# Accumulating both row halves of a projection in one PSUM bank, with ten units of queries on chip instead of eight

## The chip, the cores and the metric

The kernel runs on one core of a Trainium2 chip. The metric is device time in microseconds (us) from launch to end. Engines are named as the profile does: PE is TensorE (PEld its weight loads), DVE is VectorE, ACT is ScalarE, POOL is GpSimd, SP is the engine whose queue issues most DMAs.

## The reference

Two attention branches on the same `x` (2048 positions, width 512, 32 heads of 16) are mixed by a gate of each position:

```python
def _A_ref(x, wqkv, wo):          # window of 8 positions, step 2
    qkv = (x @ wqkv).reshape(B, S, 3, H, Dh).transpose(2, 0, 3, 1, 4)
    idx = pos[:, None] - (jnp.arange(8) * 2)[None, :]
    ...
    logits = jnp.einsum("bhsd,bhswd->bhsw", q, kg) * scale
    logits = jnp.where(mask, logits, -1e9)
    return einsum("bhsw,bhswd->bhsd", softmax(logits), vg) ... @ wo
def _B_ref(x, wq, wk, wv, wo):    # 32 query heads, one key and value head
    q, k, v = heads(x @ wq), x @ wk, x @ wv
    p = softmax(einsum("bhqd,bkd->bhqk", q, k) * scale)
    return einsum("bhqk,bkd->bhqd", p, v) ... @ wo
g = sigmoid((x * gate_w).sum(-1, keepdims=True))
return g * _A_ref(x, A_wqkv, A_wo) + (1 - g) * _B_ref(x, B_wq, B_wk, B_wv, B_wo)
```

Branch B is the large one: scores of 2048 x 2048 for 32 heads, with the exact maximum of each row taken off ahead of the exponential.

## The kernel before

The instructions are issued in an order that the program itself works out: it keeps a clock for each engine (`clk`, `free`, and constants such as `T_R` and `T_EXP`) and places work where a buffer should be free by that clock. The chip knows only the resulting order on each engine, and the semaphores between them.

**Units.** Branch B is cut into 32 units: a block of 512 queries and four heads (`NQB` x `NHG`). A unit's queries lie on chip in one of `NB` buffers `qst`, in high and low parts on both halves of the 128 rows. They are projected in the front, written to DRAM (`qd`) and brought to their buffer by `stack(u)` on SP's queue. `home(v)` says which buffer, and after which unit it is free: 8 buffers up to unit 13, then 6, since two of them (`q67`) hold half sums of keys from then on (`half_back` brings those back from DRAM).

**Row halves.** PE runs as two arrays of 64 rows, side by side: a product over 64 rows on rows 0 to 63 can run while another runs on rows 64 to 127. `b` or `odd` is the half in the code.

**The front** (about 24 to 259 us) is a list of 62 row parts (`lumps`): 14 projections of queries ("q", 2 to 15) and 48 of branch A ("a", three column groups of 16 rows blocks). Each is 12 products of 128 x 512 outputs on each half. `stream` gives each half its next product. Half 0 adds up in one PSUM bank, half 1 in the bank beside it, both for the same row part. `queries_post` copies the two banks (ACT), adds them and takes the low part off (POOL); `a_post` copies both and adds them on POOL, or every third time copies one and adds on DVE, and stores to DRAM (`ad`) from four `stage` buffers.

**Maxima.** Before a unit's exponentials, the row maxima of its scores are needed: 64 pieces of 512 keys to a unit, 2048 in all (`NF`). In between its own work, PE computes scores for them: `fill_pair` two at a time into `m2` (two banks, one DVE reduction of 1024), `fill_one` one into `m1` or `po`. Once the half sums and half differences of keys are formed (`half_sel`, `half_keys`, `half_parts`), two pieces of keys go at once: `fill_diff` computes differences and ACT takes their absolute value, `fill_sum` computes sums, and one DVE instruction adds the two and takes the maximum. In the front, `diff_ready` stops new ones at `FRONT` pieces. A unit's finished maxima go through `maxima_turn`, `shift_a` to `shift_d` into its queries' rows.

**PSUM**, eight banks: `eb[0]` and `eb[1]` (two each), `m2` (two), `m1` and `po`. The last row part of the front uses `m2`, so that the first exponentials can use `eb`.

**The main loop** has 512 steps, 16 blocks of 128 keys for each unit. A step issues two `exp_pair` (two score products side by side and one exponential of 128 x 1024 on ACT), the four products of weights and values of the step before (`weighted`, into `po`), one pair of maxima in `m2`, and, as often as `single_share` finds it due, a single one in `m1`. `single_share` spreads what is left over the steps that are left, and holds back while no further unit's queries are on chip. Output rows 0 to 7 and then 8 to 11 are projected in two breaks of the loop (`out_phase`), the last four within the last steps (`spread`). Branch A's own arithmetic runs on POOL throughout (`work`, `a_scores`, `a_values`), from DRAM.

Of the kernel before, what the change touches and what calls it, by code (L numbers as in the profile page):

```python
# [13 lines left out]
P = 128  # L14
# [21 lines left out]
NB = 8  # L36
# [7 lines left out]
FRONT = 468  # L44
# [3 lines left out]
WB = 6  # L48
# [5 lines left out]
class Banks:  # L54


    def __init__(self, tc, name):
        self.tc, self.name, self.pool, self.tiles = tc, name, None, ()
        self.whole()

    def shape(self, n):
        if len(self.tiles) != n:
            if self.pool:
                self.pool.release()
            self.pool = self.tc.alloc_tile_pool(name=self.name + "s", bufs=1, space=PSUM)
# [16 lines left out]
def gated_mix_kernel(ctx, tc, xt, wa, wk, wq, wo_a, wo_b, out):  # L82
# [16 lines left out]
    q67 = cp.tile([P, 2, 2, 512], F32R, name="q67")  # L99
    qst = [cp.tile([P, 2, 512], F32R, name=f"qst{k}") for k in range(NB - 2)] + [q67[:, 0], q67[:, 1]]  # L100
    kd = dp.tile([P, 2, 2, 512], F32, name="kd")
# [7 lines left out]
    eb = [pp.tile([P, 2, 512], F32, name=f"pe{k}") for k in range(2)]  # L109
    m1 = pp.tile([P, 512], F32, name="ps")  # L110
    po = pp.tile([P, 512], F32, name="po")
    m2 = Banks(tc, "pm")

# [25 lines left out]
    wqr = p0.tile([P, C, C, P], F32, name="wqr")  # L139
# [10 lines left out]
    def load_wq(cc, eng):  # L150
        eng.dma_start(wqr[:, cc], wq[:, cc])

    def split_wq(cc):
        cs = slice(cc * P, (cc + 1) * P)
        split(wqh[:, :, cs], wql[:, :, cs], wqr[:, cc])
# [99 lines left out]
    def parts_of():  # L255
        return p0.tile([P, 512], F32R, name="qhi", bufs=3), p0.tile([P, 512], F32R, name="qlo", bufs=2)

    def queries_post(m, bank):
# [3 lines left out]
        two = p0.tile([P, 2, 512], F32, name="two", tag="wqr", bufs=1)  # L262
        nc.scalar.activation(two, bank, AF.Copy)
        at = after("act", clk["pe"] + T_LAT, 0.92)
        own = p0.tile([P, 512], F32, name="qraw", bufs=1)
        nc.gpsimd.tensor_add(own, two[:, 0], two[:, 1])
        pool = max(pool, 1e3 * at) + 1400
        hi, lo = parts_of()

        def rest():  # L270
# [3 lines left out]
            pool = max(pool, 1e3 * after("act", 0, 0.6)) + 1400  # L274
            queries_out(m, hi, lo)
            if m > 4 and m % 2 and len(stacked) < NB:
                stack(len(stacked))

        tasks.append((pool / 1e3, rest, (), "rest"))
# [21 lines left out]
    def a_post(gg, j, x):  # L301

        nonlocal pool
        bank, key = front[x]
        settle("add", 1)
        settle("store", 2)
        own = p1.tile([P, GN], F32, name="stage", bufs=4)
        if gg == 0 and j < 3:
            two = wp.tile([P, GN], F32, name="two", tag="aext", bufs=2)
        else:  # L310
            two = p2[0].tile([P, GN], F32, name="two", tag=("", "raw", "own")[j % 3], bufs=1) if j % 3 else None
        nc.scalar.activation(own, bank[:, 0, :], AF.Copy)
        if two:
            nc.scalar.activation(two, bank[:, 1, :], AF.Copy)
        at = after("act", clk["pe"] + T_LAT, 1.05 if two else 0.52)
        free[key] = at + (0.1 if two else 1.5)

        def rest():
            nonlocal pool
            if two:  # L320
                nc.gpsimd.tensor_add(own, own, two)
                pool = max(pool, 1e3 * at) + 1280
            else:
                nc.vector.tensor_add(own, bank[:, 1, :], own)  # L324
                free[key] = after("dve", at, 0.65) + 0.1

            def store():
                for piece in a_pieces(gg):
                    a_store(own, gg, j, *piece)

            tasks.append((max(pool / 1e3, clk["dve"]) + 0.5, store, (), "store"))
            if j == NJ - 1:
                tasks.append((max(pool / 1e3, clk["dve"]) + 1.0, whole, (gg,)))

        tasks.append((at, rest, (), "add"))
# [17 lines left out]
    stacked, asked = [], set()  # L353
# [14 lines left out]
    slots = [(v, pr, t, kc) for kc in range(2) for v in range(2) for pr in range(2) for t in range(4)]  # L368
    slots += [(v, pr, t, kc) for v in range(2) for pr in range(2) for t in range(4) for kc in range(2, 4)]
    slots += [(v, pr, t, kc) for v in range(2, NU) for pr in range(2) for t in range(4) for kc in range(4)]  # L370
    half = []
    free = {"m2": 0.0, "m1": 0.0, "e0": 0.0, "e1": 0.0, "po": 0.0}
    tasks, shifted, pm = [], set(), []
# [20 lines left out]

    def to_go():
# [14 lines left out]
    def maxima_turn(v, ms):  # L410
        mt = wp.tile([P, 32], F32, name="mt")
        nc.vector.transpose(mt, ms.rearrange("p b x y -> p (b x y)"))
        tasks.append((after("dve", 0, 0.34) + (2.0 if kcd and not pe else 0.1), shift_a, (v, mt)))

    def fill_pair(dst, key):
# [3 lines left out]
        m = unit_tile(v)  # L419
        for odd in range(2):  # L420
# [5 lines left out]
    def fill_one(dst=m1, key="m1"):  # L426
# [4 lines left out]
        m = unit_tile(v)  # L431
        max_mm(dst, v, pr, t, kc, odd)
# [5 lines left out]
    sel, kcd, dd, formed, ended, wants = [], [], [], {}, set(), []  # L438
    hb = {1: (m1, po)}
# [979 lines left out]
```

## Time and profile before

| | us |
|---|---|
| three runs | 1444.36, 1444.67, 1444.96 (median 1444.67) |
| the profiled execution | 1444.01, its span 1442.2 |
| PE busy | 1435.9 |
| ACT busy | 1274.5 |
| DVE busy | 1199.8 |
| POOL busy | 1019.4 |
| first weighted product of the main loop | 259.5 |

The span runs from the first to the last instruction; the executions' time has some 2 us around it. Rows of groups read: line, engine, operation, tile written and tiles read, shapes, count; then busy us and mean ns of one; then the engine's idle time just before them and what ended it. Matmuls overlap, so their busy time is not a measure of how much PE could still take; their count in a stretch is.

### The profile page before, as it was taken

The numbers are of one execution on the slowest core, as the hardware profiler recorded it, in microseconds if no ns is written. First come the engines' busy times: TensorE is split into PE (matmuls) and PEld (weight loads), VectorE is DVE, ScalarE is ACT, GpSimd is POOL, SyncE is SP. The second block draws the span as 40 slices with busy tenths as digits, with TensorE's granted clock in tenths as the row PEclk, the third lists the DMA queues.
The fourth block names the chain that finished last, engine by engine and source line by source line (L and its number), as shares of the span: only waits on it lengthen the run. The fifth ranks groups of instructions, "written<-read, shape, count | busy, mean of one in ns | idle before, by whom it ended". The sixth has DMA issues, their size and how long they took to land.

```text
span 1442.2 us, 29203 instructions
## 1 busy us (share of the span) xinstructions
PE 1435.9 (100%) x10524; PEld 674.7 (47%) x10524; DVE 1199.8 (83%) x1878; ACT 1274.5 (88%) x1596; POOL 1019.4 (71%) x1796
## 2 busy tenths in 40 slices
PE   9999999999999999999999999999999999999998
PEld 7977777433333333333333476333333337333343
DVE  8978889688888888888898888888888888889812
ACT  6659888999999999999999888999999998999986
POOL 7952989878898988888988897888888815111121
PEclk9999999999999999999999999999999999999999
DMA  7753433122021120212322200221202011000110
GB/s 241 220 156 103 130 98 104 56 62 90 14 87 43 46 90 13 72 42 69 97 77 73 85 31 31 83 61 43 72 13 72 12 42 35 9 2 2 28 33 30
DMA packets 107457, 96.12 MB, mean 67 GB/s; under 512 B 84976, under 2 KB 89120, under 8 KB 103088
## 3 DMA queue, kind: packets, MB, share of 16 engines
q1 hardware_dynamic: 100224, 55.04, 14.2%
q0 software_dynamic: 6368, 37.90, 7.9%
q8 instruction: 83, 1.36, 0.4%
q10 hardware_dynamic: 720, 1.31, 0.3%
q14 instruction: 62, 0.51, 0.1%
HBM read 63.18 MB, written 30.49 MB: 65 GB/s over the span
## 4 chain that ended last, share of the span: by engine, by line
PE 99%; DVE 1%; ACT 0%; issue 0%; POOL 0%; DVEq 0%; ACTq 0%; POOLq 0%
PE po L592 35%; PE pe L582 24%; PE pe L1218 12%; PE pm L393 8%; PE ps L393 6%; PE pe L890 5%; PE pm L491 3%; PE ps L491 2%; PE pm L944 1%; PE po L491 1%; PE pe L227 1%; PE po L193 0%; PE po L393 0%; PE pm L1218 0%; PE po L1043 0%; PE ps L1043 0%
## 5 line engine op out<-in xcount | busy, mean ns | idle before, releaser
L584 ACT ACTIVATE pexp<-pe 128x1024 f32<-128x1024 f32 x1022 | 987.2, 1022 | 81.7 <-PE pe L582 78.8
L422 DVE TENSOR_REDUCE mx<-pm 128x2 f32<-128x1024 f32 x508 | 621.0, 1223 | 131.0 <-PE pm L393 125.6
L592 PE MATMUL po<-pexp,vst 128*32 128x512 f32 x4096 | 545.5, 605 | 0.0
L582 PE MATMUL pe<-qst,kst 64*128 64x512 f32 x1916 | 442.2, 451 | 0.4
L582 PEld LDWEIGHTS pe<-qst,kst 64*128 64x128 f32 x1916 | 179.8, 183 | 474.8 <-ACT pexp L584 466.8
L433 DVE TENSOR_REDUCE mx<-ps 128x1 f32<-128x512 f32 x414 | 281.6, 680 | 3.3 <-PE ps L393 3.3
L393 PE MATMUL pm<-kst,qst 62*128 62x512 f32 x980 | 201.3, 396 | 0.1
L656 POOL TENSOR_TENSOR pr<-aext 128x256 f32<-128x256 f32 x256 | 182.0, 737 | 3.0 <-DMA aext<-ad 2.7
L716 POOL TENSOR_TENSOR oa<-oa,av 128x256 f32<-128x256 f32 x224 | 164.0, 732 | 15.4
L393 PE MATMUL ps<-kst,qst 62*128 62x512 f32 x406 | 160.0, 394 | 0.0
L592 PEld LDWEIGHTS po<-pexp,vst 128*32 128x32 f32 x4096 | 80.5, 108 | 166.4 <-issue 157.0
L713 POOL TENSOR_TENSOR av<-aext,lg 128x256 f32<-128x256 f32 x224 | 139.3, 622 | 13.1
L520 ACT ACTIVATE dd<-pm 128x512 f32<-128x512 f32 x180 | 101.5, 606 | 16.4 <-PE pm L491 8.9
L1218 PE MATMUL pe<-wah,xl 64*128 64x512 f32 x376 | 109.9, 393 | 0.0
L1218 PE MATMUL pe<-wal,xh 64*128 64x512 f32 x376 | 108.1, 393 | 0.0
L1218 PE MATMUL pe<-wah,xh 64*128 64x512 f32 x376 | 107.5, 395 | 0.4 <-DVE stage L324 0.3
L393 PEld LDWEIGHTS pm<-kst,qst 62*128 62x128 f32 x980 | 96.9, 186 | 2.8 <-DVE mx L422 0.6
L662 POOL TENSOR_TENSOR tr<-pr 128x512 f32<-128x512 f32 x64 | 81.8, 1278 | 4.4
L520 ACT ACTIVATE pexp<-pm 128x512 f32<-128x512 f32 x116 | 65.0, 600 | 15.3 <-PE pm L491 8.8
L662 POOL TENSOR_TENSOR tr<-tr 128x256 f32<-128x256 f32 (+1 forms) x128 | 72.4, 566 | 8.2
L393 PEld LDWEIGHTS ps<-kst,qst 62*128 62x128 f32 x406 | 75.8, 187 | 3.7 <-issue 1.2
L537 DVE CUSTOM_DVE_ANT_0 dd<-po,dd 128x512 f32<-128x512 f32 x90 | 62.1, 690 | 12.5 <-PE po L491 7.3
(221 smaller groups left out, 1913.8 us busy)
## 6 DMA issues: line engine op xcount, KB each, us to landing
aext<-ad POOLq DMA_DIRECT2D x32, 1056.0 KB, 5.7
qst<-qd SPq DMA_DIRECT2D x60, 128.0 KB
ad<-stage SPq DMA_DIRECT2D x32, 240.0 KB
qd<-qhi SPq DMA_DIRECT2D x16, 256.0 KB
qd<-qlo SPq DMA_DIRECT2D x16, 256.0 KB
td<-raw SPq DMA_DIRECT2D x32, 128.0 KB
oa<-td SPq DMA_DIRECT2D x256, 16.0 KB
xraw<-xt SPq DMA_DIRECT2D x15, 256.0 KB
```

What stands on the lines that cost most here:

```text
L393: nc.tensor.matmul(dst, qst[home(v)[0]][b:b + 62, pr, t * P:(t + 1) * P], kst[b:b + 62, kc * 512:(kc + 1) * 512], start=True, stop=True)
L422: nc.vector.tensor_reduce(m[:, :, pr, t, kc], dst, AX.X, ALU.max)
L433: nc.vector.tensor_reduce(m[:, odd, pr, t, kc:kc + 1], dst, AX.X, ALU.max)
L520: nc.scalar.activation(d[:, odd], m2[:, odd, :], AF.Abs)
L582: nc.tensor.matmul(bank[:, odd, :], kst[b:b + 64, kt * P:(kt + 1) * P], qst[home(u)[0]][b:b + 64, pr, :], start=True, stop=True)
L584: nc.scalar.activation(e, bank, AF.Exp, scale=SCALE)
L592: nc.tensor.matmul(po[32 * i:32 * i + 32, :], vst[:, kt, :], pexp[s, i // 2][:, i % 2, :], start=(kt == 0), stop=(kt == NJ - 1))
L656: nc.gpsimd.tensor_mul(pr[:, k], q, e[:, o:o + NH, AC:2 * AC])
L662: nc.gpsimd.tensor_add(nx, cur[:, :, 0:n], cur[:, :, n:2 * n])
L713: nc.gpsimd.tensor_mul(av, e[:, o:o + NH, 2 * AC:].rearrange("p j (h d) -> p j h d", d=DH), lg[:, w].unsqueeze(3).to_broadcast([P, NH, AG, ...
L716: nc.gpsimd.tensor_add(ao, ao, av)
L1218: nc.tensor.matmul(front[2 if x == last else x % 2][0][:, b, :], l[h], r[h], start=(i == 0), stop=(i == 3 * C - 1))
```

## The change

Both halves of a row part now add up in the same bank. Half 0's 12 products come first, half 1's 12 follow into the same sums; meanwhile half 0 does the next row part. `front_stream` takes the place of `stream` in the front, with four banks, one row part each (`front_bank`). Half 1 may start a row part only once the program's order proves that half 0's last product of it is complete: `mark` notes at each product that waits for a freed bank which earlier products must be done (`known`), and `may` asks for it. One copy by ACT empties a bank; for queries a second copy gives the high part. No addition is left.

`NB` is 10: six buffers of their own and four in branch A's pool (`kept`, `held`), which is laid over the query weights when the query projections are done. Units 6 to 9 are stacked in the first row parts of branch A. `kept` and `held` later serve as an output block and as the second half of branch A's results, so POOL's second pass waits for step 161. The half sums have a buffer of their own (`kcd`), with no way through DRAM. They are formed at "q" 11 and 13 instead of "a" 0, 4 and 0, 6, both in `m2`. `FRONT` is 596 instead of 468. `stage` has two buffers instead of four, `wah` and `wal` have eight instead of six. The second exponential of step 0 is issued after the front's last copy. The first output phase no longer waits for a small lead of the maxima, and a later one waits for it alone.

```diff
-NB = 8
+NB = 10
-FRONT = 468
+FRONT = 596
-WB = 6
+WB = 8
...
-        return (v % NB, v - NB) if v < 2 * NB - 2 else ((v - NB) % (NB - 2), v - NB + 2)
+        return (v % NB, v - NB) if v < 2 * NB - 4 else ((v - NB) % (NB - 4), v - NB + 4)
...
+    eb = [Banks(tc, "pe0", 2, "right"), Banks(tc, "pe1", 2)]
...
     def queries_post(m, bank):
-        nc.scalar.activation(two, bank, AF.Copy)
-        nc.gpsimd.tensor_add(own, two[:, 0], two[:, 1])
+        nc.scalar.activation(own, bank, AF.Copy)
+        nc.scalar.activation(hi, bank, AF.Copy)
         def rest():
-            nc.scalar.activation(hi, own, AF.Copy)
             nc.gpsimd.tensor_sub(lo, own, hi.bitcast(F32))
...
+    def a_post(gg, j, bank):
+        settle("store", 1)
+        own = p1.tile([P, GN], F32, name="stage", bufs=2)
+        nc.scalar.activation(own, bank, AF.Copy)
+        at = after("act", clk["pe"] + T_LAT, 0.52)
...
+    def mark(*keys):
+        known[0] = max([known[0]] + [seen[k] for k in keys if k in seen])
+        seen.update({k: issued[0] for k in keys})
+        issued[0] += 1
...
-            if lump == ("a", 0, 3):
+            if lump == ("q", 10):
                 half_sel()
-            elif lump in (("a", 0, 4), ("a", 0, 6)):
-                wants.append(1 if lump[2] == 4 else 0)
+            elif lump in (("q", 11), ("q", 13)):
+                wants.append(1 if lump[1] == 11 else 0)
...
-        nc.tensor.matmul(front[2 if x == last else x % 2][0][:, b, :], l[h], r[h], start=(i == 0), stop=(i == 3 * C - 1))
+        if b == 0 and i == 0:
+            mark(f"f{x % 4}")
+        nc.tensor.matmul(front_bank(x), l[h], r[h], start=(b == 0 and i == 0), stop=(b == 1 and i == 3 * C - 1))
+        (ends_at if b == 0 else seen)[x if b == 0 else f"f{x % 4}"] = issued[0]
...
+    def may(b, at):
+        x, i = at
+        if b == 0:
+            if i == 0 and x - 4 >= posted[0]:
+                return False
+            lump = lumps[x]
+            return lump[0] == "q" or (lump[1], i // 3) in wal
+        return i > 0 or known[0] >= ends_at[x]
...
+    def front_stream(seq):
+        while min(at) < len(seq):
+            ...
+            for b in sorted((0, 1), key=lambda b: b not in lone):
+                if b in lone:
+                    lone[b]()
+                elif at[b] < len(seq) and (b == 0 or at[0] // n > at[1] // n) and may(b, seq[at[b]]):
+                    dur = max(dur, mm(b, seq[at[b]]))
+                    at[b] += 1
...
+        if lump == ("a", 0, 0) and i == 2:
+            queries_done()
+        if lump[0] == "a" and lump[1] == 0 and lump[2] in (1, 3, 5, 7) and i == 2:
+            stack(len(stacked))
+        if x == last and i == 5:
+            exp_pair(0, 0)
...
+    def queries_done():
+        settle("rest", 0)
+        p0.release()
+        branch_a()
+        for k in range(NB - 4, NB):
+            clear(k, nc.gpsimd)
...
-            yield lambda: g < 8 or p2b
+            yield lambda: (g < 8 or p2b) and (not hf or step[0] > 16 * NB + 1)
...
-        if s == 16 * NB + 4:
-            half_back()
...
-        elif due or ... (lead < LEAD or s >= 16 * (NHG * (k + 2) + 1)):
+        elif due or ... (not outs or lead < LEAD):
```

More of the change, by code (lines that the diff above doesn't have):

```diff
@@ L299, in a_store, with store @@
         nc.sync.dma_start(dst, src)
[L301 to L335, printed above, removed]
+    def a_post(gg, j, bank):
[3 more added lines that the diff above has]
+        at = after("act", clk["pe"] + T_LAT, 0.52)
+        def store():
+            for piece in a_pieces(gg):
+                a_store(own, gg, j, *piece)
+        tasks.append((at + 0.5, store, (), "store"))
+        if j == NJ - 1:
+            tasks.append((at + 1.0, whole, (gg,)))
     def gates():
@@ L412, in maxima_turn @@
         nc.vector.transpose(mt, ms.rearrange("p b x y -> p (b x y)"))
[L413 removed]
+        tasks.append((after("dve", 0, 0.34) + (2.0 if formed and not pe else 0.1), shift_a, (v, mt)))
     def fill_pair(dst, key):
@@ L846, in stream @@
             lone = {}
-            if wants and all(free[k] <= clk["pe"] + 0.1 for k in (("m1", "po") if wants[0] else ("m2",))):
-                half_keys(wants.pop(0))
             halves = groups or any(pend) or paired() and not half
-            if halves or 1 in wants:
+            if halves:
                 for b in range(2):
@@ L858, in stream @@
                 lone[half[0][4] if half else 0] = lambda: fill_one(m1, "m1")
-            elif pooled and fillable() and free["po"] <= clk["pe"] - just():
-                lone[half[0][4] if half else 0] = lambda: fill_one(po, "po")
             dur = 0.0
@@ new lines, in front_bank @@
+    def front_bank(x):
+        return eb[(1, 1, 0, 0)[x % 4]][:, x % 2, :]
+    def may(b, at):
[7 more added lines that the diff above has]
+    def front_stream(seq):
+        n = 3 * C
+        at, told, idle = [0, 0], 0, 0
+        while min(at) < len(seq):
+            lone = {}
+            if wants and free["m2"] <= clk["pe"] + 0.1:
+                half_keys(wants.pop(0))
+            halves = groups or any(pend) or paired() and not half and not ended
+            if halves:
+                for b in range(2):
+                    if sum_ready(b):
+                        lone[b] = lambda b=b: fill_sum(b)
+                    elif diff_ready(b):
+                        lone[b] = lambda b=b: fill_diff(b)
+                        break
+            else:
+                for dst, key in ((m1, "m1"), (po, "po")):
+                    if not lone and fillable() and free[key] <= clk["pe"] - just():
+                        lone[half[0][4] if half else 0] = lambda dst=dst, key=key: fill_one(dst, key)
+            dur = 0.0
+            for b in sorted((0, 1), key=lambda b: b not in lone):
+                if b in lone:
+                    now = clk["pe"]
+                    lone[b]()
+                    clk["pe"] = now
+                elif at[b] < len(seq) and (b == 0 or at[0] // n > at[1] // n) and may(b, seq[at[b]]):
+                    dur = max(dur, mm(b, seq[at[b]]))
+                    at[b] += 1
+            if lone or dur:
+                idle = 0
+                after("pe", 0, T_R)
+            else:
+                idle += 1
+                assert idle < 400
+                clk["pe"] += 0.05
+                run_tasks()
+            if not (ended or wants or halves) and slots and fillable() and free["m2"] <= clk["pe"] - just():
+                clk["pe"] = max(clk["pe"], free["m2"])
+                fill_pair(m2, "m2")
+            while told < min(at):
+                told += 1
+                done_mm(seq[told - 1])
@@ L1254, in whole @@
         ready_gg += 1
-    front = [(eb[1], "e1"), (eb[0], "e0"), (m2, "m2")]
-    stream([(x, i) for x in range(len(lumps)) for i in range(3 * C)], mm, done_mm, True, 3 * C * lumps.index(("a", 0, 0)))
-    assert not groups and not any(pend)
+    def queries_done():
+        nonlocal pool
+        settle("rest", 0)
[3 more added lines that the diff above has]
+            clear(k, nc.gpsimd)
+        pool = max(pool, 1e3 * clk["pe"]) + 9000
+    free.update({f"f{k}": 0.0 for k in range(4)})
+    front_stream([(x, i) for x in range(len(lumps)) for i in range(3 * C)])
+    while groups or any(pend):
+        for b in range(2):
+            if sum_ready(b):
+                fill_sum(b)
+            elif diff_ready(b):
+                fill_diff(b)
+        clk["pe"] += T_R
     formed.clear()
-    for kind in ("add", "store"):
-        settle(kind, 0)
+    settle("store", 0)
     while [t for t in tasks if len(t) > 3]:
```

162 lines of the change are left out of this document (89 added, 73 removed).

## The prediction

> **What bounds the kernel now.** I read the clock and the chain first, then busy time by stretches, then the matmuls of the front alone, and last single steps of the main loop in order of time. The chain of the end is TensorE's almost alone, and the rows by stretches (columns: time, then busy us and count of PE, weight loads, DVE, ACT, POOL, then granted clock, DMA share, GB/s) show a clock of 1.00 throughout.
>
> ```profile
> PE 99%; DVE 1%; ACT 0%; issue 0%; POOL 0%; DVEq 0%; ACTq 0%; POOLq 0%
> ```
>
> ```profile
> 25.00:50.00 25.00, 25.00 (x218) 23.53 (x216) 24.67 (x32) 17.44 (x46) 21.77 (x19) 1.00 0.60 163
> 75.00:100.00 25.00, 24.99 (x198) 19.43 (x196) 19.95 (x32) 12.56 (x29) 13.41 (x14) 1.00 0.52 144
> ...
> 200.00:225.00 25.00, 25.00 (x215) 18.86 (x213) 22.48 (x68) 21.64 (x42) 23.54 (x35) 1.00 0.46 132
> ```
>
> A busy PE of 25.00 says little; the count says more. 218 half-array matmuls (64 rows) in 25 us is 0.1147 us for one, 0.229 us for two side by side. From 200 to 225 us it is 215, so the front runs at 99% of its own best rate. The work in it, matmuls from 25 to 259 us by form (count after the x):
>
> ```profile
> L1218 PE MATMUL pe<-wah,xl 64*128 64x512 f32 x376 | 109.9, 393 | 0.0
> ...
> L491 PE MATMUL pm<-kcd,qst 62*128 62x512 f32 x138 | 53.9, 397 | 0.2 <-ACT dd L520 0.2
> L1218 PE MATMUL pe<-xh,wql 64*128 64x512 f32 x112 | 29.2, 391 | 0.0
> ...
> L491 PE MATMUL pm<-kcd,q 62*128 62x512 f32 x42 | 16.4, 397 | 0.0
> L393 PE MATMUL pm<-kst,qst 62*128 62x512 f32 x54 | 15.5, 395 | 0.0
> L393 PE MATMUL po<-kst,qst 62*128 62x512 f32 x26 | 10.3, 396 | 0.0
> L393 PE MATMUL ps<-kst,qst 62*128 62x512 f32 x25 | 10.0, 398 | 0.0
> ...
> L1218 PE MATMUL pm<-wah,xl 64*128 64x512 f32 x8 | 2.8, 391 | 0.0
> ```
>
> Projections stand in three rows of 376, three of 112 and three of 8 (one of each is shown): 1488, or 62 row parts of 24. Maxima: 54+26+25 plain ones, 138+42 by differences in `pm` and as many by sums in `ps` and `po`: 465 of the 468 that FRONT names (a few records are missing). 1488+468 = 1956 times 0.1147 is 224.4 us, and eight whole-array products of half sums add 1.8. The projections span 23.8 to 258.5 us:
>
> ```profile
> L1218 PE MATMUL pe<-xh,wqh x112: 385/390/498, 23.8 to 71.8; 64*128 64x512 f32 x112
> ...
> L1218 PE MATMUL pm<-wah,xl x8: 388/391/394, 255.5 to 258.5; 64*128 64x512 f32 x8
> ```
>
> So about 8.5 us of the front's 234.7 are lost, the largest piece where row x198 stands (half sums, pool of branch A).
>
> In the main loop the four weighted products open each step's end. A step with a single maximum (`ps`) and one without:
>
> ```profile
> 600.45 1.07 PE L592 MATMUL po<-pexp,vst 128*32 128x512 f32 x8
> 602.24 0.40 PE L393 MATMUL ps<-kst,qst 62*128 62x512 f32 x1
> 602.57 1.06 PE L592 MATMUL po<-pexp,vst 128*32 128x512 f32 x8
> 604.16 3.84 ACT L584 ACTIVATE pexp<-pe 128x1024 f32<-128x1024 f32 x4 [0.18 <-PE pe L582]
> 604.46 1.06 PE L592 MATMUL po<-pexp,vst 128*32 128x512 f32 x8
> 606.59 1.07 PE L592 MATMUL po<-pexp,vst 128*32 128x512 f32 x8
> ```
>
> With a single: 602.57-600.45 = 2.12 us, TensorE's time. Without: 604.46-602.57 = 1.89 us, ScalarE's time, since four exponentials in a row take 3.84, or 1.92 for a step. So a single costs 0.23 us there, and this much is to be had until ScalarE is reached. The groups of the page agree (idle time stands behind the second bar), and so do the waits from 262 to 1432 us (us in total, times, longest):
>
> ```profile
> L584 ACT ACTIVATE pexp<-pe 128x1024 f32<-128x1024 f32 x1022 | 987.2, 1022 | 81.7 <-PE pe L582 78.8
> L422 DVE TENSOR_REDUCE mx<-pm 128x2 f32<-128x1024 f32 x508 | 621.0, 1223 | 131.0 <-PE pm L393 125.6
> L433 DVE TENSOR_REDUCE mx<-ps 128x1 f32<-128x512 f32 x414 | 281.6, 680 | 3.3 <-PE ps L393 3.3
> ```
>
> ```profile
> ACT pexp L584 <- PE pe L582: 78.1, 376, 0.5
> ```
>
> 78.1/376 = 0.208 us that ScalarE idles for each single. I take 0.215, between 0.208 and 0.23.
>
> **The change part by part.**
>
> *128 maxima move from the main loop to the front.* FRONT goes from 468 to 596 of 2048, with ten units on chip instead of eight; both leave 44 of the units on chip over (512-468, 640-596). The main loop places one pair in nearly every step before 480 and fills up with singles by what is left to do, so the 128 are singles: of 414 in the `ps` row some 25 are the front's, and 389 become about 261. Gain: 128 x 0.215 = 27.5 us. Bounds: 29.4 by 0.23; 20 if a quarter of the steps cannot take their pair because units are late. That is possible: home 0 serves unit 16 only after step 176, so up to step 180 at most 16 units, 1024 maxima, exist, of which 596+360 go as pairs; the 68 left are 0.38 singles a step against 0.5 wanted, which only moves 20 singles later.
>
> *What they cost in the front.* Nothing hides them: its rate is at 99%. 128 x 0.1147 = +14.7 us. The halves a lone maximum leaves go to a projection there, so it pays for one half and not two as in the main loop; this difference is the whole gain. Whether the vector engines keep up: maxima come as half sums, one |.| on ScalarE and one fused sum and maximum on DVE for two maxima. Half sums now form at row parts 9 and 11 of 62 instead of 18 and 20. An estimate of the maxima before that: DVE is busy 24.67 of 25 us with plain ones, at 0.61 (1223/2) to 0.68 us each, so some 40 in 25 us and 52 in the first 32. 544 come after, or 10.3 in each of 53 row parts: a row part takes (24+10.3) x 0.1147 = 3.93 us and holds 5.1 fused maxima. These follow each other in 0.70 us, though their row and that of the accumulator's read add up to 0.77:
>
> ```profile
> 205.39 0.69 DVE L537 CUSTOM_DVE_ANT_0 dd<-po,dd 128x512 f32<-128x512 f32 x1
> ...
> 206.01 0.08 DVE L537 DVE_READ_ACCUMULATOR2_ANT mx<- 128x1 f32 x1
> ...
> 206.08 0.69 DVE L537 CUSTOM_DVE_ANT_0 dd<-ps,dd 128x512 f32<-128x512 f32 x1
> ```
>
> ```profile
> L520 ACT ACTIVATE dd<-pm 128x512 f32<-128x512 f32 x180 | 101.5, 606 | 16.4 <-PE pm L491 8.9 <-PE pe L1218 2.6 <-PE ps L491 1.1
> L312 ACT ACTIVATE stage<-pe 128x512 f32<-128x512 f32 x47 | 28.1, 598 | 9.5 <-PE pe L1218 6.2 <-POOL stage L321 2.3 <-issue 0.7
> ```
>
> DVE: 5.1 x 0.70 = 3.6 of 3.93 us, 92%; it is 90% now (22.48 of 25). ScalarE: one copy of 0.6 instead of two, 5.1 x 0.6 for |.|, so 3.7 of 3.93 at most, while copies and |.| overlap. It fits, with little over.
>
> *One bank for both halves.* The second copy and the addition go:
>
> ```profile
> L321 POOL TENSOR_TENSOR stage<-stage,two 128x512 f32<-128x512 f32 x31 | 40.4, 1304 | 23.4 <-ACT two L314 22.9 <-issue 0.5
> ...
> L314 ACT ACTIVATE two<-pe 128x512 f32<-128x512 f32 x31 | 18.7, 604 | 1.6 <-DVE sel L451 1.6
> ...
> L266 POOL TENSOR_TENSOR qraw<-two 128x512 f32<-128x512 f32 x14 | 18.1, 1292 | 1.1
> ...
> L324 DVE TENSOR_TENSOR stage<-pe,stage 128x512 f32<-128x512 f32 x16 | 11.0, 686 | 2.7 <-ACT stage L312 2.7
> ```
>
>  TensorE at 99% covers all of it, so it is worth nothing by itself; what it buys is the room on ScalarE above. New is that half two of a row part may start only when half one is known to be complete, which a later maximum's freed bank tells. Half one works a row part ahead, with four banks to run in. Cost: at the start half two, and at the end half one, has no projection for 12 x 0.1147 = 1.4 us, and one turn of a bank (0.70) comes on top at one end: +3.4 us. Bounds: 0, if maxima take the idle half; 8.3, if half one runs three row parts ahead at both ends (2 x 36 x 0.1147). 3.4 is the distance that steady filling keeps.
>
> *The seam to the main loop.* Now both exponentials of step 0 run before the last copy:
>
> ```profile
> 256.61 1.03 ACT L584 ACTIVATE pexp<-pe 128x1024 f32<-128x1024 f32 x1 [0.33 <-PE pe L582]
> 258.00 1.03 ACT L584 ACTIVATE pexp<-pe 128x1024 f32<-128x1024 f32 x1 [0.36 <-PE pe L582]
> 258.92 0.59 ACT L312 ACTIVATE stage<-pm 128x512 f32<-128x512 f32 x1
> ```
>
> After the change the second needs the bank pair that the last row part fills, so it follows the copy: one exponential of 1.0 us later. +1.0 (0 to 2).
>
> *Queues.* The loads of units 6 to 9 move on SP's queue from the query row parts into the first row parts of branch A. They write into buffers laid over the query weights, which POOL clears first (945 ns a piece, two to a unit), after the last low parts have left by DMA. SP is in order, so the first store stands behind that, ScalarE's next copy behind the store, since `stage` has two buffers instead of four, and |.| behind the copy. Once, 0 to 2 us: +0.5. In steady state a store has two row parts, 7.9 us, and no longer waits for POOL. Removing the 1.0 MB return of half sums (`q67`) and the order of output rows 0 to 11 cost nothing: the first output phase waits for unit 15 and turned rows, which POOL, with 58 us (40.4+18.1) less to do, has no later.
>
> ```profile
> L197 POOL MEMSET qst<- 32x1024 f32 x10 | 9.5, 945 | 0.5
> ```
>
> **Sum.** -27.5 + 14.7 + 3.4 + 1.0 + 0.5 = -7.9 us. The profiled execution took 1444.0 us (span 1442.2), 0.7 below the median of 1444.7. 1436.1 on its scale, 1436.8 as a median.
>
> [...]
>
> **The rivals.**
>
> *The added maxima are free.* Weight loads were busy 18.86 of 25 us from 200 to 225 us and 23.53 from 25 to 50 us. If that difference were idle TensorE time, the 128 would fit into it: -27.5+4.9 = -22.6, 1422. Against it: the counts differ by 1% only (215 and 218). [...] 5%.
>
> *Slower: the hand-over between the halves.* If half two waits in each row part for a bank's turn (0.70 us) while half one stands at its fourth bank, a row part loses 0.35 us of the array: 62 x 0.35 = 22 us, 1458. It decides from 0.13 us a row part (7.9/62). For it: maxima that prove completion come 0.38 us apart at best, and a queue in order stops with them. Against: half one may run up to three row parts ahead, so a lag is paid once. 11%.
>
> *No change: DVE sets the front.* If the fused maximum costs 0.77, 5.1 x 0.77 + 0.2 (turning of maxima, branch A's rows) = 4.1 us a row part against 3.93, over 53 row parts +9: 1445.7. The spacing of 0.70 speaks against it; so tight a fit speaks for it. The same end has a main loop that gains only 20. 14%.
>
> *The losses of the front shrink.* Four banks instead of two, no meeting of the halves at the first row part of branch A: of the 8.5 us lost up to 5 come back, 1432. Row x198 speaks for it, that much of it is the half sums themselves against it. 15%.
>
> **The numbers.** The forecast has 55% (its own range 1433 to 1441), the last rival 15%, free maxima 5%, no change 14%, slower 11%. 0.2%, or 2.9 us, is what a measurement of this kernel can tell from no change. Faster: 55+15+5 = 75%. The range from 1428 to 1447 leaves out free maxima and most of the slower case.
>
> **What would show it.** The front's projections end at 274 to 282 us instead of 258.5, with 596 maxima in it; 215 or more half matmuls in 25 us. Single maxima in `ps` fall to about 285 in all; ScalarE's idle time before exponentials falls from 78.8 to about 52 us; steps of 1.89 to 1.92 us become nearly half of those before step 480. Wrong, if idle time appears before projections behind ScalarE's copies or DVE's maxima, if DVE in the front is above 96%, or if the loop keeps its number of singles.

## The result and the profile after

The changed kernel takes 1461.74 us (median, 1461.2 to 1462.3) where the kernel before takes 1444.64 in the same runs: a ratio of 1.0118 (95% interval 1.0101 to 1.0136), 17.1 us slower. The span grew by 18.3 us. Three marks divide it: the first weighted product of the main loop starts at 294.05 us instead of 259.51 (+34.5); from there to the last step's weighted products it is 1154.7 instead of 1172.1 (-17.4); the end is 11.8 instead of 10.6 (+1.2). The granted clock of TensorE was 1.00 in the whole front and, but for one stretch of 3.4 us shown below, in the main loop.

The front by stretches (columns as before: time, busy us and count of PE, weight loads, DVE, ACT, POOL, then clock, DMA share, GB/s):

```profile
25.00:50.00 25.00, 25.00 (x198) 23.53 (x198) 24.98 (x33) 13.22 (x44) 10.87 (x10) 1.00 0.51 140
50.00:75.00 25.00, 25.00 (x197) 19.76 (x195) 15.79 (x32) 14.23 (x28) 12.51 (x12) 1.00 0.66 190
...
150.00:175.00 25.00, 23.68 (x190) 16.00 (x188) 20.54 (x61) 19.82 (x39) 17.20 (x34) 1.00 0.60 173
...
200.00:225.00 25.00, 25.00 (x216) 18.50 (x212) 23.03 (x70) 22.56 (x44) 23.15 (x38) 1.00 0.43 119
225.00:250.00 25.00, 24.82 (x184) 15.49 (x182) 20.16 (x60) 19.33 (x36) 16.46 (x34) 1.00 0.31 88
250.00:275.00 25.00, 24.24 (x188) 15.32 (x184) 20.50 (x63) 19.73 (x39) 17.16 (x39) 1.00 0.21 55
```

From 200 to 225 us all is as forecast: 216 half matmuls, within 1% of the most that any stretch of before had (218). Behind it the count falls to 184 and 188, and no engine is full: DVE falls to 20 of 25 us, ScalarE to 19 to 20, POOL to 17. Nothing is short of throughput, so something waits in a ring. PE's and ScalarE's waits from 25 to 294 us (total us, times, longest) name it:

```profile
PEld pm L474 <- ACT dd L504: 27.5, 87, 1.6
PEld po L474 <- DVE mx L522: 7.0, 42, 0.2
PEld ps L474 <- DVE mx L522: 6.0, 37, 0.2
```

```profile
ACT dd L504 <- DVE mx L522: 9.5, 26, 0.9
```

L474 issues products of half differences (into `pm`) and half sums (into `po`, `ps`), L504 is ScalarE's absolute value, L522 DVE's fused sum and maximum. In the front of before, the first of these rows reads 4.4 us, 21 times, 0.5 at most:

```profile
PEld pm L491 <- ACT dd L520: 4.4, 21, 0.5
```

One turn of the ring in the changed kernel, in order of time (start, length, engine; in brackets the idle time ahead and what ended it):

```profile
231.72 0.68 DVE L522 CUSTOM_DVE_ANT_0 dd<-po,dd 128x512 f32<-128x512 f32 x1
231.93 1.17 ACT L504 ACTIVATE dd<-pm 128x512 f32<-128x512 f32 x2
...
233.16 0.18 PEld L474 LDWEIGHTS pm<-kcd,kept 62*128 62x128 f32 x1
233.17 0.69 DVE L522 CUSTOM_DVE_ANT_0 dd<-ps,dd 128x512 f32<-128x512 f32 x1 [0.76 <-ACT dd L504]
...
233.96 1.21 ACT L504 ACTIVATE dd<-pm 128x512 f32<-128x512 f32 x2 [0.86 <-DVE mx L522]
```

DVE idles 0.76 us until ScalarE has written a `dd`; it then reads and frees it by 233.86, and ScalarE, which idled 0.86 us for a free `dd`, writes the next two. Each waits for the other in turn, and TensorE, in order, stands at a difference whose half of `pm` ScalarE has not emptied. `dd` has two buffers of two halves: four differences ahead of their sums, and all are held. Up to four the program's plan allows (`diff_ready`). Counted by the order of the matmuls, 1.4 to 2.4 differences stand ahead of their sums on the mean in stretches of 20 us of before, and four only now and then; here it is 3.4 to 3.6 from 220 to 280 us.

In the main loop the groups of the page moved the forecast way, but not as far (idle time behind the second bar):

```profile
L569 ACT ACTIVATE pexp<-pe 128x1024 f32<-128x1024 f32 x1022 | 983.9, 1022 | 66.6 <-PE pe L567 62.2
...
L425 DVE TENSOR_REDUCE mx<-ps 128x1 f32<-128x512 f32 x285 | 193.7, 680 | 0.0
```

Single maxima fell from 414 to 285, the number forecast; ScalarE's idle time ahead of exponentials from 78.8 to 62.2, not to 52. The first output phase takes 71.9 us, where before it was 67.5. The step behind it takes 3.44 us, 1.3 more than a usual one: the granted clock was 0.50 from 917.24 to 920.66 us, and its weighted products took 1.94 us instead of 1.06.

```profile
915.83 0.49 PE L474 MATMUL po<-kcd,qst 62*128 62x512 f32 x1 [0.19 <-DVE mx L522]
...
917.22 1.94 PE L577 MATMUL po<-pexp,vst 128*32 128x512 f32 x8
...
920.66 1.06 PE L577 MATMUL po<-pexp,vst 128*32 128x512 f32 x8
```

### The profile page after: what moved, and what is told of

Read it like the earlier page. It is cut to its first block, busy times and chain, and to the rows that moved or that the text cites. A ratio compares the mean times of both kernels' runs of the same rounds, so it can differ in the third digit from the quotient of the medians.

```text
span 1460.5 us, 29289 instructions
## 1 busy us (share of the span) xinstructions
PE 1447.3 (99%) x10524; PEld 676.1 (46%) x10524; DVE 1149.9 (79%) x1876; ACT 1298.6 (89%) x1653; POOL 964.5 (66%) x1747
## 4 chain that ended last, share of the span: by engine, by line
PE 96%; DVE 1%; ACT 1%; POOL 1%; issue 1%; ACTq 0%; DVEq 0%; POOLq 0%
PE po L577 35%; PE pe L567 24%; PE pe L1205 11%; PE pm L375 8%; PE pm L474 4%; PE ps L375 4%; PE pe L882 4%; PE ps L474 2%; PE po L474 2%; PE pm L936 1%; PE pe L231 1%; ACT dd L504 0%; DVE dd L522 0%; DVE pexp L522 0%; PE po L197 0%
## 5 line engine op out<-in xcount | busy, mean ns | idle before, releaser
L569 ACT ACTIVATE pexp<-pe 128x1024 f32<-128x1024 f32 x1022 | 983.9, 1022 | 66.6 <-PE pe L567 62.2
L567 PE MATMUL pe<-qst,kst 64*128 64x512 f32 x1788 | 424.0, 456 | 1.6 <-ACT pexp L569 0.8
L425 DVE TENSOR_REDUCE mx<-ps 128x1 f32<-128x512 f32 x285 | 193.7, 680 | 0.0
L504 ACT ACTIVATE dd<-pm 128x512 f32<-128x512 f32 x264 | 151.0, 600 | 30.7 <-DVE mx L522 9.5
L704 POOL TENSOR_TENSOR oa<-oa,av 128x256 f32<-128x256 f32 x224 | 164.2, 733 | 15.5
L1205 PE MATMUL pe<-wah,xl 64*128 64x512 f32 x384 | 135.2, 399 | 0.0
L1205 PE MATMUL pe<-wal,xh 64*128 64x512 f32 x384 | 133.7, 396 | 0.8 <-POOL wal L123 0.8
L1205 PE MATMUL pe<-wah,xh 64*128 64x512 f32 x384 | 131.2, 397 | 0.1
L474 PE MATMUL pm<-kcd,qst 62*128 62x512 f32 x280 | 112.1, 406 | 1.7 <-ACT dd L504 1.3
L375 PE MATMUL ps<-kst,qst 62*128 62x512 f32 x272 | 107.3, 395 | 0.0
L522 DVE CUSTOM_DVE_ANT_0 dd<-ps,dd 128x512 f32<-128x512 f32 x132 | 91.0, 690 | 18.1 <-PE ps L474 11.7
L522 DVE CUSTOM_DVE_ANT_0 dd<-po,dd 128x512 f32<-128x512 f32 x132 | 91.1, 690 | 17.4 <-PE po L474 12.0
```

The lines of the kernel that those rows point to most:

```text
L375: nc.tensor.matmul(dst, qst[home(v)[0]][b:b + 62, pr, t * P:(t + 1) * P], kst[b:b + 62, kc * 512:(kc + 1) * 512], start=True, stop=True)
L425: nc.vector.tensor_reduce(m[:, odd, pr, t, kc:kc + 1], dst, AX.X, ALU.max)
L474: nc.tensor.matmul(dst, qst[home(v)[0]][b:b + 62, pr, t * P:(t + 1) * P], kcd[b:b + 62, kc // 2, x, :], start=True, stop=True)
L504: nc.scalar.activation(d[:, odd], m2[:, odd, :], AF.Abs)
L522: nc.vector.tensor_tensor_reduce(d[:, odd], dst, d[:, odd], 1.0, -FMAX, ALU.add, ALU.max, m[:, odd, pr, t, kc:kc + 1])
L567: nc.tensor.matmul(bank[:, odd, :], kst[b:b + 64, kt * P:(kt + 1) * P], qst[home(u)[0]][b:b + 64, pr, :], start=True, stop=True)
```

## The experiments

The theory: the change itself is worth something; the loss is the ring of `dd`, entered because the plan puts four differences ahead of their sums, with smaller losses in the new front. The rivals: the front is too full for ScalarE and DVE; or the arrangement with one bank is slow by itself.

**Fewer differences ahead (e1_depth).** In the front a difference is placed only when its half has none open, so two at most:

```diff
 def diff_ready(odd):
     ...
-    return all(x[1] is not d for x in pend[odd])
+    return not pend[odd] if not pe else all(x[1] is not d for x in pend[odd])
```

> The changed kernel with one limit more: in the front a new difference is issued only when its half has no difference whose sum is still to come, so at most two stand ahead of their sums instead of four. 587 maxima in the front instead of 589, nothing else moves. Theory lag: the changed front stalls because its order runs differences so far ahead that the absolute value on ScalarE has to wait for DVE to give back one of the two buffers, and the next difference, in order on TensorE, waits with it. Then the wait of differences for the absolute value falls from 27.5 us to under 10, the first weighted product comes at 282 to 286 us instead of 294, and the time is 1449 to 1454. Theory throughput: DVE and ScalarE deliver a fused maximum only every 0.84 us in the front, whatever the order (the kernel before had the same pace). Then the waits move elsewhere and the first weighted product stays at 291 or later: 1458 to 1462.

1447.09 us, ratio 1.0018 (1.0009 to 1.0027): 14.6 us of the loss are gone by an edit of the order alone, with 587 maxima in the front instead of 589. The main loop starts at 282.56 instead of 294.05, so 11.5 us of them are the front's. The first output phase, which the edit does not limit, is 68.7 us instead of 71.9 (in its new order four stand ahead at 2% of the half products), and no stretch of front or loop ran at half clock. The waits of e1_depth in the front and the stretch that had 184:

```profile
PEld pm L474 <- ACT dd L504: 2.8, 8, 1.1
```

```profile
225.00:250.00 25.00, 25.00 (x216) 18.25 (x216) 23.99 (x72) 21.86 (x43) 20.19 (x47) 1.00 0.27 71
```

DVE is now busy 23.99 of 25 us, with 35 fused maxima of 0.69 us (each has a second, short record), and TensorE runs at 216. So the engines do have the throughput that the prediction gave them; DVE at 96% was no bound here. The rival of a front too full falls.

**A third pair of buffers (e2_three) and its control (e3_wb7).** The order stays that of the control; only the ring is longer. Both have seven weight buffers instead of eight, which makes the room:

```diff
-WB = 8
+WB = 7
 # e2_three only, once branch A's buffers are laid out:
+dd.append(p2[0].tile([P, 2, 512], F32, name="dd3", bufs=1))
 # e2_three only, in diff_ready, so that the order of the control stays:
-    return all(x[1] is not d for x in pend[odd])
+    return (len(pend[odd]) < 2 or bool(pe)) and all(x[1] is not d for x in pend[odd])
```

> The changed kernel with a third pair of buffers for absolute values from branch A's first row part on, and with seven instead of eight buffers for split weights to make room for it. Orders of instructions are those of the run with seven buffers alone, differences up to four ahead. Theory lag: only the wait of ScalarE for DVE's buffer is taken away, so the stalls go: first weighted product 4 to 10 us earlier than in the run with seven buffers alone. Theory throughput: no difference (under 2 us).

> The changed kernel with seven instead of eight buffers for split weights, the control for the third pair of buffers: both theories say within 4 us of the changed kernel's 1461.7, stalls as there.

1456.67 (ratio 1.0083, 1.0069 to 1.0097) against 1463.11 (1.0129, 1.0115 to 1.0143). A third pair brings 6.4 us with the order unchanged; the main loop starts 8.8 us earlier (290.86 against 299.62). The row of the ring, e2_three and then e3_wb7:

```profile
PEld pm L474 <- ACT dd L504: 6.6, 25, 1.1
```

```profile
PEld pm L474 <- ACT dd L504: 23.9, 82, 0.5
```

That the buffers are what is waited for is shown by this pair. The clock does not make the difference: each of the two traces has two stretches of 3.4 us at 0.50 in the front or at its end (from 218.6 and 290.3 us in e2_three, 148.7 and 298.9 in e3_wb7), and the mean granted clock is 0.998 in both. That a better order is worth more than a third buffer is not shown: e1_depth, whose main loop starts at 282.56, has eight weight buffers, and one less costs 3.7 us in e10_stage4 below.

**How many ahead (e11_lag3, e13_lag3_all).** At most three, in the front alone, and then everywhere:

```diff
-    return all(x[1] is not d for x in pend[odd])
+    return (bool(pe) or sum(map(len, pend)) < 3) and all(x[1] is not d for x in pend[odd])   # e11_lag3
+    return sum(map(len, pend)) < 3 and all(x[1] is not d for x in pend[odd])                 # e13_lag3_all
```

> The changed kernel with at most three differences ahead of their sums instead of four (e1_depth had two). Lag theory: the loss grows with the lag; at a mean of 2.5 to 2.6 in the last 15 row parts, between 1.6 and 3.6, a difference often finds its buffer still held, so between the two: 1450 to 1457. Rival (the gain of e1_depth came by other changes of the order, not by the lag): 1459 to 1463. If three is as good as two (1446 to 1449), the stall sets in only where both buffers of both halves are held.

1451.39, ratio 1.0052 (1.0038 to 1.0065), inside the lag theory's range, but not for its reason. The front is as good as with two (main loop from 282.79):

```profile
PEld pm L474 <- ACT dd L504: 5.3, 19, 1.5
```

So the loss does not grow evenly with the lag: it sets in where all four halves are held, and one free half is enough. The rest stood in the first output phase, which this kernel leaves unlimited: 72.5 us, against 68.7 in e1_depth. There too differences run ahead, four ahead at 16% of its half products (19% in the changed kernel, 0 before). Waits for ScalarE's absolute value in that phase, before, after and e11_lag3:

```profile
PEld pm L491 <- ACT pexp L520: 1.1, 6, 0.2
```

```profile
PEld pm L474 <- ACT pexp L504: 7.8, 30, 0.5
```

```profile
PEld pm L474 <- ACT pexp L504: 7.0, 25, 0.5
```

> The kernel of e11_lag3 with the same limit (three differences ahead) in the output phases and the main loop too, not in the front alone. Theory (the longer first output phase is the same stall: four ahead): that phase falls from 72.5 to 67.5 to 69 us and its row of differences waiting for ScalarE from 7.0 to 2 us or less, so 3 to 5 us below e11_lag3's 1451.4: 1446.4 to 1448.4. Rival (that phase is longer for its output products or for the turn of its banks): it stays at 71 to 73, 1450.5 to 1452.

1447.73, ratio 1.0027 (1.0018 to 1.0036). The phase takes 68.2 us, and its row is

```profile
PEld pm L474 <- ACT pexp L504: 1.5, 8, 0.2
```

The same ring held the output phase, worth 4.3 us of the phase and 3.7 between the medians. The rival, that the phase grew by its own work, falls: it has 156 half products in the kernel before, in the changed one and here.

**The limit on the kernel before (e12_before_lag).** The same edit as e1_depth's, on the kernel before.

> The kernel before with the lag limit of e1_depth; its front then holds 449 maxima instead of 468. Lag theory: with a mean lag of 1.6 to 2.3 the kernel before loses 0.3 to 1.1 us in 20, so the limit has nothing to take away, and 19 maxima go to the main loop at 0.06 each: 1445 to 1446.5. Rival (the limit is simply a better order and the kernel before gains from it too): 1438 to 1443.

1447.98, ratio 1.0031 (1.0022 to 1.0041). Both theories miss: the limit helps by 1.2 us at most, near what the lag theory had, but costs 3.5 us in all instead of about 1. Its front holds 449 maxima and ends 3.4 us sooner (the 19 alone are 2.2); the main loop has 411 singles instead of 389 and is 7.4 us longer. Of these some 2.0 us stand in the two output phases, the first step and one step of 2.8 us; what is left is 0.25 us for each of the 22. So a limit is not a better order as such.

**One bank, with the old number of maxima (e5_pace).** e1_depth, with the front's maxima held to 470, spread over it:

```diff
-... or not pe and NF - to_go() >= FRONT):
+... or not pe and NF - to_go() >= min(FRONT, 34 + 7.1 * posted[0])):
```

> One bank for both halves without the added maxima: the changed kernel with at most one difference ahead per half (as in e1_depth), and with the front's maxima held to 34 + 7.1 for each finished row part, 470 in all against the 468 of the kernel before. Single maxima in the main loop 416 by the order against 414 before, so the main loop's should cost the same within 3 us. Theory overhead (stagger of the halves at both ends, seam, later start of half sums): the front ends 7 to 10 us after the 259.5 of before, by nothing but that, time 1451 to 1455; then the 117 maxima moved by e1_depth are worth 4 to 8 us net. Rival: the overhead grows with the added maxima and is small without them: front ends at 260 to 263, time 1444 to 1448.

1456.60, ratio 1.0087 (1.0073 to 1.0101). With 470 maxima against 468 before, the main loop starts at 270.7 instead of 259.5: the arrangement costs 11.2 us in the front, 12.2 in all. Where, by its stretches:

```profile
25.00:50.00 25.00, 25.00 (x195) 23.15 (x197) 24.54 (x33) 13.03 (x42) 10.61 (x10) 1.00 0.51 132
50.00:75.00 25.00, 25.00 (x197) 19.91 (x195) 15.86 (x30) 14.18 (x30) 13.23 (x12) 1.00 0.66 194
...
150.00:175.00 25.00, 22.85 (x184) 17.58 (x182) 15.36 (x46) 14.79 (x29) 16.05 (x32) 0.93 0.57 170
```

Before, these stretches have 218, 217 and 216. At 0.1147 us each that is 2.6, 2.3 and 3.7 us; the others up to 250 us give 2.1 back. At the start half one runs alone (26 half matmuls in the first 5 us instead of 42: 1.8 us), and at the end half two (44 in the last 8 us before the last projection starts instead of 68: 2.8 us); the seam behind it, to the first weighted product, is 3.2 us instead of 1.0. From 54 to 57 and 64 to 65 us the half sums are formed; before had its own loss for them at 76 to 80, where this kernel waits 1.2 us for POOL's low weights instead. The stretch at 150 us holds one pause: ScalarE's copy waits for one of two `stage` buffers,

```profile
ACT stage L308 <- DMA ad<-stage: 3.2, 1, 3.2
```

whose store was issued just behind two loads of 1056 KB (these landed at 157.3 and 160.9 us, the copy could start at 161.9), and TensorE stands behind the absolute value that follows it. Then its matmuls are slower for 3.4 us, at a granted clock of 0.50 from 163.7 to 167.1:

```profile
160.50 0.39 PE L1205 MATMUL pe<-wah,xl 64*128 64x512 f32 x1
163.05 0.49 PE L474 MATMUL pm<-kcd,qst 62*128 62x512 f32 x1 [2.15 <-ACT dd L504]
...
165.31 0.62 PE L1205 MATMUL pe<-wal,xh 64*128 64x512 f32 x1
```

The loss from 160 to 180 us is 4.2 us here and 1.4 in e1_depth, whose pause is shorter. Against e1_depth this kernel also shows what the added maxima are worth: 117 more in the front cost 11.9 us there, or 14.7 without that difference (0.101 to 0.126 each), and save 21.5 in the loop (0.184 each).

**Fewer singles and nothing else (e4_drop).** The kernel before without 128 of the main loop's single maxima (a part of the scores of units 16 to 31 is left out of the maximum).

> The kernel before, with 128 maxima left out of units 16 to 31 (8 of 64 in each), so that the main loop has about 118 single maxima fewer and some pairs fewer while the front is untouched: the price of single maxima in the main loop alone. What is left out isn't computed. Price of 0.215 us as predicted: 1444.6-27.5 = 1417 (1415 to 1420). If the price is what the changed kernel's main loop shows (17.4 us for 119): 1424 to 1428. If output phases grow by 5 us whenever fewer maxima are left, their first one takes 72 us instead of 67.5.

1423.82, ratio 0.9858 (0.9843 to 0.9873): -20.7 us for 118 singles fewer in the records, 0.176 each, where the prediction had 0.215. The groups show why not more:

```profile
L584 ACT ACTIVATE pexp<-pe 128x1024 f32<-128x1024 f32 x1022 | 983.4, 1023 | 66.7 <-PE pe L582 63.3
...
L433 DVE TENSOR_REDUCE mx<-ps 128x1 f32<-128x512 f32 x296 | 201.3, 680 | 2.8 <-PE ps L393 2.8
```

ScalarE's idle time falls by 15.5 us (78.8 to 63.3), just as in the changed kernel. Steps outside the breaks take 27.6 us less, with one step of 2.1 us fewer among them: 0.216 each, the prediction's price. But the breaks grow by 6.7 us (that step included): one of 6.9 us at step 263 is new. There pairs of maxima stand one behind the other, in the banks of the exponentials too, as the code's `pause` does when a unit's maxima come short of its turn, and TensorE waits for DVE to empty the banks; the step behind it takes 3.6 us, at a granted clock of 0.50 from 800.0 to 803.4:

```profile
793.73 0.49 PE L393 MATMUL pe<-kst,qst 62*128 62x512 f32 x2
...
799.01 0.74 PE L582 MATMUL pe<-qst,kst 64*128 64x512 f32 x4 [1.76 <-DVE mx L422]
799.68 1.66 PE L592 MATMUL po<-pexp,vst 128*32 128x512 f32 x8
```

So 0.176 is no clean price of a single: it holds a break that this edit brought with it.

**Mending what is left (e6_seam, e14_seam_lag3, e7_best, e8_tail, e9_early, e10_stage4).** e6_seam stands on e1_depth, and the others on e6_seam; e14_seam_lag3 has the limit of e13_lag3_all in place of e1_depth's, e8_tail stands on e7_best and e10_stage4 on e9_early. e6_seam issues the second exponential of step 0 as soon as no difference is open, ahead of the last copy, with `pm` as its banks:

```diff
+if x == last and i > 6 and not groups and not any(pend) and (0, 1) not in pexp:
+    exp_pair(0, 1, True)
```

> e1_depth with one move: the second exponential of step 0 goes into the maxima's two banks as soon as these are free, ahead of the front's last copy, as in the kernel before, instead of behind it into the banks of the last row parts. If the seam costs what the trace of e1_depth shows between the last projection and the first weighted product (279.4 to 282.6, against 258.5 to 259.5 before), 2.0 us come back: 1445 to 1445.5. If that time was only the end of half one's lone row part, it stays within 0.5 us of 1447.1.

1444.99, ratio 1.0004 (0.9995 to 1.0013). The seam gives 2.1 us back and the kernel ties with before; no kernel here that computes everything is faster than before.

> The kernel of e6_seam (early second exponential) with the limit of three everywhere instead of two in the front. Theory: the front as in e6_seam (a limit of three was as good as two there), the first output phase 67.5 to 69: 1444.2 to 1446.3, a tie with the kernel before. Rival (three ahead still costs in the front where the half sums and stores disturb it): 1447 to 1449.

1446.17, ratio 1.0017 (1.0009 to 1.0026), at the edge of the theory's range: the output phase is 68.2 as expected, and the front 1.1 us longer than e6_seam's, with three maxima more.

e7_best adds to e6_seam two things: the first weights of branch A are loaded and split two row parts earlier, and singles are spread evenly up to step 176. e8_tail lets maxima go on into the last row part as well; e9_early has the earlier weights alone:

```diff
-            ahead_wa(0, m - 4)
+            ahead_wa(0, m - 2)                                          # e7, e8, e9
+            if s < 176:
+                rate = min(rate, (64 * 16 - NF + to_go()) / (180 - s) - 2)   # e7, e8
-        if x == last - 1 and i == 3 * C - 6:
+        if x == last and i == 3:                                        # e8
```

> e6_seam, and two more: weights of branch A are split two row parts earlier, so that its first row part doesn't wait for POOL (1.5 us of loss at 76 to 78 us in e1_depth), and before step 176 single maxima of the main loop are spread evenly up to the landing of unit 16 (so that fewer steps without a single follow one another; these had 18 of 205 at 2.12 us instead of 1.90). 590 maxima in the front. Expected 1440 to 1444: -2 for the seam, -1.5 for the weights, -1 to -2 for the spreading. Rival: runs of steps without a single are limited by ScalarE on average and spreading brings nothing, 1443 to 1445.

> e7_best with maxima going on into the last row part of the front (until half one's third product of it) instead of ending in the one before. 592 maxima in the front instead of 590, and the lone half one at the end has company. If the idle half at the end (271 to 279 us, 5 half matmuls in a us instead of 8.7) can be filled, 1 to 3 us less than e7_best; if the last maxima only push out the seam, the same or 1 us more.

> The kernel with the lag limit and the early second exponential, and the low parts of branch A's first weights made two row parts ahead on GpSimd instead of four. Theory (what is lost in the front adds up and is not given back): the wait of TensorE for the low weights at 76 to 78 us (1.2 us, and 0.5 beside it) goes, so 1443.3 to 1444.4. Rival (the next late thing takes its place, or the end of the program gives it back): 1444.6 to 1446.5.

1446.47 (1.0017, 1.0008 to 1.0025), 1447.85 (1.0026, 1.0016 to 1.0036) and 1446.16 (1.0011, 1.0002 to 1.0020). The low weights are no longer waited for, and the loss from 60 to 80 us falls by 1.4 us, yet the front ends at 280.72 us in e9_early and 280.73 in e6_seam: four maxima more, and 0.8 us lost at 100 to 120 us. The first output phase, which takes what is due, is 71.2 us with 172 half products instead of 68.4 with 148, and the end 11.9 instead of 10.8. So e9_early's rival holds. e7_best lies above both of its ranges, and e8_tail is 1.4 us slower than e7_best, a little more than its rival allowed: neither spreading singles nor filling the idle half brought anything.

> The kernel of e9_early with four staging buffers for the half-one and half-two copies instead of two, and seven weight buffers instead of eight to make room. Theory: ScalarE's copy at 161 us no longer waits 1.1 us for a store to leave, and the difference behind it not 1.2 us, so 1.0 to 1.5 below e9_early: 1442 to 1443.4. Rival (the store is late for the loads beside it, and something else waits for it): as e9_early within 0.8. One weight buffer less is taken to cost nothing: it was 1461.7 with eight and 1463.1 with seven in runs on different chips, so up to 1.3 worse is possible.

```diff
-WB = 8
+WB = 7
-        own = p1.tile([P, GN], F32, name="stage", bufs=2)
+        own = p1.tile([P, GN], F32, name="stage", bufs=4)
```

1450.51, ratio 1.0042 (1.0030 to 1.0055): theory and rival both missed. The loss from 160 to 180 us does fall, from 1.6 to 0.3 us, but from 120 to 225 us new waits stand, for weights that come later with seven buffers than with eight:

```profile
PEld pe L1205 <- ACT wah L119: 2.4, 2, 1.2
PEld pe L1205 <- POOL wal L123: 1.9, 2, 1.1
```

The front is 3.7 us longer. That one weight buffer less costs nothing was wrong; four `stage` buffers with eight of weights were not tried.

## Why the prediction was wrong

Three differences of medians account for the 17.1 us: the arrangement +12.2 (e5_pace against before), the move of 117 maxima -9.5 (e1_depth against e5_pace), the ring of `dd` +14.6 (after against e1_depth: 11.5 in the front, 3.2 in the first output phase, 1.3 in the step at half clock behind it, and 1.5 less in the second output phase, 34.6 against 36.1). The sum is +17.3.

*The move: mechanism right, size a quarter off.* Forecast -27.5 + 14.7 = -12.8; measured -21.5 + 11.9 = -9.6. The front's price of 0.1147 was good (0.101 to 0.126). The loop's 0.215 was mis-sized for the whole loop: 0.184 here, and 0.176 in e4_drop with its new break. Outside the breaks e4_drop pays 0.216, so two steps give the price of a step rightly, but it holds only while the steps around them stay as they are: of the steps with a pair alone 18 of 205 take over 2.05 us in e1_depth, 6 of 96 before. Only 121 of the 128 moved. The bound of 20 us was nearer, but not for its reason: it was for steps that cannot take their pair, and the loop has 480 pairs in e1_depth as before.

*One bank: mis-sized.* Forecast 3.4 + 1.0 + 0.5 = 4.9, measured 12.2 (9.4 without the longer pause at 161 us). The stagger, put at 3.4, was 1.8 + 2.8 = 4.6 us, inside its bounds: a half without a partner issues 5 products in 1 us, where two side by side issue 8 to 9. The seam, put at +1.0, was +2.2 (3.2 us instead of 1.0), since the second exponential waits behind the copy and the products behind both. The stage queue, put at 0.5, costs 0.9 to 3.7 more than before at 160 to 180 us, at a store beside two loads, not in the first row parts where it was looked for. These three make 7.7 to 10.5 us; the 1.7 left were not told apart.

*"It fits, with little over" is the step that failed.* It compared busy time with the row part's time for each engine alone, and that comparison was right: from 225 to 250 us e1_depth runs 5 fused maxima in a row part at 0.69 us and TensorE at 216. What it left out is the ring between the engines: TensorE in order, two halves of `pm`, two pairs of `dd`. It was in the trace of before, as the row of 4.4 us in 21 waits, and the code's condition lets four go ahead. The term was put at nothing and was 11.5 us in the front. That the denser maxima are what pushes the plan to four is likely and not shown: no run has the old number of maxima in the new front without a limit. The prediction listed as a sign of error idle time before projections; it came before differences, one queue entry earlier.

*The slower rival* gave 1458, near the measured time, by luck and the wrong mechanism: the hand-over of a bank from half one to half two costs nothing in steady state, as 216 half matmuls from 200 to 225 us show. Half one is always in another bank than half two; no run has both at work in the same one, so what that would do is not shown. *DVE sets the front* falls with e1_depth: the fused maximum holds 0.69. *Free maxima* falls with the 0.101 us or more that each added one costs in the front: in e1_depth weight loads are busy 18.25 of 25 us from 225 to 250 us, where TensorE runs at 216 half matmuls, so their busy share does not show room for maxima here. *The losses of the front shrink* was the reverse of what happened.

What stays open: the end of the program is 10.6 to 10.9 us in some kernels (before, e1_depth, e6_seam) and 11.5 to 12.2 in others (after, e9_early, e13_lag3_all), with the same last computations; the difference lies behind DVE's last sum and was not followed. Nor was it tried whether a front without the stagger of the halves is possible.

## What to carry to other kernels

An engine that has the time for its work can still stall: where an order fixed ahead couples three engines through two buffers, follow the ring once round, and ask how many pieces the plan puts in flight and how many the buffers hold; here, at four pieces on four halves, differences waited 27.5 us in the front, and with one piece fewer 5.3 (e11_lag3). When a denser stretch is planned, look up in the old trace the wait that the density multiplies, however small it is there. Price a piece of work by moving a hundred of them, not by the difference of two steps alone, and look at the breaks and at the granted clock before the difference is divided by a hundred.

## What the runs showed of the hardware

The ring is a cliff, not a slope: waits of differences for ScalarE in the front are 2.8 us with two differences ahead at most (e1_depth), 5.3 with three (e11_lag3) and 27.5 with four (the changed kernel). In e1_depth DVE was busy 23.99 of 25 us (96%) from 225 to 250 us, and TensorE ran at 216 half matmuls there. Two row halves that accumulate into one bank, one behind the other, ran at 216 half matmuls in 25 us (the changed kernel, 200 to 225 us), as two banks did before (216 from 150 to 175 us). A lone half ran at 5 in 1 us (the first 5 us of the front in e5_pace), 0.2 us each against 0.1147 side by side.

In e5_pace TensorE stood for 2.15 us ahead of 163.05 us, and the granted clock, 1.00 up to then, was 0.50 from 163.7 to 167.1 us; a half matmul took 0.62 us instead of 0.39. With both, the loss from 160 to 180 us is 4.2 us. A pause of 1.13 us at the same place in the changed kernel has a clock of 1.00 behind it. At the end of the first output phase of the changed kernel, with 16 matmuls from 913.83 to 917.24 us and no pause over 0.21 us among them, the clock was 1.00, and from 917.24 to 920.66 us it was 0.50. In e4_drop it was 0.50 from 800.0 to 803.4 us, where the wait ahead was 1.76 us. What lowers the clock these runs do not show.
